# Two-bank PSUM tiles, small operations moved from ScalarE to VectorE, and the first FFN block in two halves, in a top-k attention and SwiGLU kernel

## The chip, the cores and the metric

The kernel runs on one core of one Trainium2 chip. The metric is the device time in microseconds (us) of one execution, and less is better. Engines are named as in the profile: PE (TensorE matmuls), PEld (TensorE weight loads), DVE (VectorE), ACT (ScalarE), POOL (GpSimd) and SP (SyncE, which issues nearly all DMAs).

## The reference

Two parts, one after the other. B=8 batches, H=8 heads, S=576 tokens, D=64, and an FFN with 512 and 1536 columns.

```python
scores = scale * (q @ k.T)                       # per batch and head, 576 x 576
kth    = np.partition(scores, -32)[..., -32]     # the 32nd largest of each row
attn   = softmax of scores, those below kth left out, with eps 1e-9 in the sum
x      = (attn @ v), heads side by side          # (4608, 512)
out    = (silu(x @ w_gate) * (x @ w_val)) @ w_out
```

q, k and v are float32. The three weight matrices are float64 in memory, and the kernel has to round them to float32 itself.

## The kernel before, in words

**Attention units.** A unit is one batch, one tile of 128 query tokens and one pair of heads. There are 8 x 5 x 4 = 160 units. Of each five query tiles the last has 64 tokens: it is worked as "one head" (the two heads share the partitions), so its unit has half of the work. A unit goes through these functions: `scores` (PE matmuls into PSUM, ACT copies to `sc`), `select` (top-32 on DVE: four rounds of MAX8, with three rounds of MATCH_REPLACE8 between them, for each head 7 operations), `penalize` (ACT: `top`, Relu; POOL: `bias`, subtract), `weigh` (ACT: Exp with its row sum, then the 1e-9), `normalize` (DVE reciprocal, ACT multiply), `turn` (PE transposes of `e` into `etps`, ACT copies to `et`) and `values` (PE matmuls into `av`, ACT copies to `xT`, for two units at a time). `prep` transposes q and k of a head pair once for each batch.

**The main loop.** Iteration n runs `select` of unit n, `penalize` and `weigh` of unit n-1, `normalize` and `turn` of unit n-2, and in even iterations `values` of units n-4 and n-3 and the `scores` of units n+1 and n+2. The program is emitted in one order, and the last lines of the kernel tie each engine to that order. So each engine runs its own list strictly in order, and waits where an operand or a buffer isn't ready.

**FFN blocks and pieces.** The 4608 tokens are 18 blocks of 256. `feed(kb)` is a generator that emits a block in pieces. A piece of the two products is 4 matmuls of 256 columns; on the chip each is two records (fp32 goes in two passes). ACT reads the products out of PSUM (Tanh, scale, add, copy), through a list `on_act`; POOL multiplies them, through `on_pool`. Blocks 1 to 17 then take 42 matmuls of 256 columns with differences of the output weights; block 0 takes the output weights as they are (`o_ps`, matmuls of 512 columns, 12 for each 128 tokens). A block can start when all heads of its tokens are in `xT` (`done`). In each iteration `share(n)` gives the number of pieces that may be emitted, and `pieces(k)` puts them at three places of the iteration, with what is left at its end. When no block is ready, nothing is emitted.

**Rounding the weights.** `rounded` treats a piece of 128 x 512 float64 weights: a DMA into `w` (three buffers), three ACT operations (L114 Abs of the high words, L116 the low words, L117 sign), a DVE shift (L121), and on POOL an integer add (L122) and the product with the sign (L123). There are 36 pieces: 24 for w_gate and w_val, 12 for w_out. `weights` is stepped from the main loop by `rounding(1)`, in the six `select` operations in the middle of an iteration, five times in six: 5 steps for each iteration of a full unit, 2 steps to a piece, so 2.5 pieces in an iteration. `ready[0]` counts the pieces that are rounded; `need` in `feed` steps the generator on by itself if a product is to be emitted before its weights.

**PSUM.** Five single banks `ps_t` serve scores, transposes, `av` and `prep`; three banks `ps_f` serve the FFN.

## Time and profile before

| what | before |
|---|---|
| median of 3 runs (lowest to highest) | 1851.85 us (1851.02 to 1856.61) |
| the profiled execution, its own time | 1851.39 us |
| its span in the profile | 1849.6 us |
| PE busy | 1703.3 us, 92% of the span |
| DVE busy | 1452.7 us, 79% |
| ACT busy | 1422.8 us, 77% |
| POOL busy | 1042.9 us, 56% |

The busy shares are means over stages that differ. Sections of the page: (1) engines, (2) 40 slices of the span, each digit a busy share in tenths, (4) the chain of work that ended last, (5) groups of instructions by line, with the mean time of one and the idle time before them. A timeline line gives start, duration, engine, line, operation, output and inputs, the number of merged instructions, and in brackets the idle time before it and what ended it. A duration holds the whole latency of an instruction; in a row of like instructions the distance from one start to the next is shorter.

### The profile page before, as it was taken

The numbers are of one execution on the slowest core, as the hardware profiler recorded it, in microseconds if no ns is written. First come the engines' busy times: TensorE is split into PE (matmuls) and PEld (weight loads), VectorE is DVE, ScalarE is ACT, GpSimd is POOL, SyncE is SP. The second block draws the span as 40 slices with busy tenths as digits, with TensorE's granted clock in tenths as the row PEclk, the third lists the DMA queues.
The fourth block names the chain that finished last, engine by engine and source line by source line (L and its number), as shares of the span: only waits on it lengthen the run. The fifth ranks groups of instructions, "written<-read, shape, count | busy, mean of one in ns | idle before, by whom it ended". The sixth has DMA issues, their size and how long they took to land.

```text
span 1849.6 us, 31170 instructions
## 1 busy us (share of the span) xinstructions
PE 1703.3 (92%) x11012; PEld 1401.3 (76%) x11012; DVE 1452.7 (79%) x3084; ACT 1422.8 (77%) x3329; POOL 1042.9 (56%) x1058
## 2 busy tenths in 40 slices
PE   4448899899999999999999999999999999999999
PEld 3336668687888878887888877887788878788878
DVE  6886888997998788887988877887888888788300
ACT  6898788788788787788887886878787877787632
POOL 4777755545575636564556535565556554556444
PEclk7668999899999999999999999999999999999999
DMA  6433130001200020001200020000300010000000
GB/s 181 118 91 92 34 79 14 12 1 31 63 1 13 12 68 14 12 1 28 65 13 1 12 68 25 1 13 2 90 1 13 1 43 25 1 12 12 1 12 12
DMA packets 109309, 59.70 MB, mean 32 GB/s; under 512 B 88544, under 2 KB 96992, under 8 KB 109152
## 3 DMA queue, kind: packets, MB, share of 16 engines
q1 hardware_dynamic: 108016, 57.37, 11.9%
q8 instruction: 87, 1.43, 0.3%
q14 instruction: 70, 0.57, 0.1%
q10 hardware_dynamic: 1136, 0.33, 0.1%
HBM read 48.23 MB, written 9.44 MB: 31 GB/s over the span
## 4 chain that ended last, share of the span: by engine, by line
PE 71%; ACT 15%; POOL 8%; issue 2%; DMA 1%; DVE 1%; SPq 1%; POOLq 0%; ACTq 0%
PE f L477 36%; PE av L421 8%; PE x_ps L563 8%; PE s L308 6%; PE etps L387 5%; PE y_ps L563 5%; POOL e L351 3%; ACT e L360 2%; ACT e L348 2%; ACT e L375 2%; ACT sc L313 2%; PE s L294 1%; ACT et L388 1%; PE kqps L263 1%; POOL size L122 1%
## 5 line engine op out<-in xcount | busy, mean ns | idle before, releaser
L328 DVE MAX8 m<-e 128x8 f32<-128x576 f32 x864 | 615.2, 748 | 3.3
L351 POOL TENSOR_TENSOR e<-sc,e 128x576 f32<-128x576 f32 x288 | 403.1, 1419 | 329.9 <-ACT e L348 329.9
L332 DVE MATCH_REPLACE8 e<-m,e 128x576 f32<-128x576 f32 x576 | 423.9, 742 | 0.0
L477 PE MATMUL f<-xT,wg 128*128 128x256 f32 x1728 | 403.7, 383 | 0.0
L477 PE MATMUL f<-xT,wv 128*128 128x256 f32 x1728 | 403.4, 383 | 0.0
L477 PEld LDWEIGHTS f<-xT,wg 128*128 128x128 f32 x1728 | 325.3, 192 | 51.4 <-issue 8.1
L477 PEld LDWEIGHTS f<-xT,wv 128*128 128x128 f32 x1728 | 325.9, 192 | 50.4 <-issue 8.3
L505 POOL TENSOR_TENSOR h<-h,half_g 128x512 f32<-128x512 f32 x108 | 137.9, 1277 | 227.2 <-ACT h L504 226.4
L387 PE MATMUL etps<-ident,e 128*128 128x128 f32 (+1 forms) x1312 | 189.9, 287 | 78.6 <-ACT e L375 63.3
L360 ACT ACTIVATE e<-e,bias 128x576 f32<-128x576 f32 x288 | 221.2, 771 | 49.6 <-POOL e L351 46.1
L387 PEld LDWEIGHTS etps<-ident,e 128*128 128x128 f32 (+1 forms) x1312 | 157.9, 147 | 117.4 <-ACT e L375 84.5
L328 DVE MAX8 m<-sc 128x8 f32<-128x576 f32 x288 | 203.5, 744 | 45.0 <-ACT sc L299 25.3
L308 PE MATMUL s<-kqT 64*128 64x288 f32 x1024 | 180.8, 460 | 39.6 <-ACT sc L313 24.2
L348 ACT ACTIVATE e<-sc,top 128x576 f32<-128x576 f32 x288 | 209.4, 769 | 5.2
L332 DVE MATCH_REPLACE8 e<-m,sc 128x576 f32<-128x576 f32 x288 | 211.9, 742 | 0.0
L375 ACT ACTIVATE e<-e,tot 128x576 f32<-128x576 f32 x288 | 208.8, 770 | 0.0
L510 POOL TENSOR_TENSOR h<-h,val 128x512 f32<-128x512 f32 x108 | 137.8, 1276 | 106.3 <-ACT val L509 94.9
L388 ACT COPY et<-etps 128x512 f32<-128x512 f32 (+1 forms) x448 | 183.3, 490 | 7.3 <-PE etps L387 6.5
L313 ACT COPY sc<-s 128x288 f32<-128x288 f32 x512 | 164.3, 403 | 15.6 <-PE s L308 15.6
L308 PEld LDWEIGHTS s<-kqT 64*128 64x128 f32 x1024 | 102.8, 197 | 86.6 <-ACT sc L313 30.0
L421 PE MATMUL av<-et,v 128*64 128x128 f32 (+1 forms) x2560 | 158.4, 267 | 0.0
L421 PEld LDWEIGHTS av<-et,v 128*64 128x64 f32 x2560 | 136.8, 140 | 7.5 <-ACT top L344 3.4
(74 smaller groups left out, 2000.3 us busy)
## 6 DMA issues: line engine op xcount, KB each, us to landing
v<-in_v_dram SPq DMA_DIRECT2D x32, 256.0 KB, 3.2
kq_in<-in_k_dram SPq DMA_DIRECT2D x63, 128.0 KB, 2.8
kq_in<-in_q_dram SPq DMA_DIRECT2D x63, 128.0 KB, 3.0
w<-in_moe_w_gate_dram SPq DMA_DIRECT2D x12, 512.0 KB, 3.7
w<-in_moe_w_val_dram SPq DMA_DIRECT2D x12, 512.0 KB, 3.7
w<-in_moe_w_out_dram SPq DMA_DIRECT2D x12, 512.0 KB, 3.6
out_dram<-o SPq DMA_DIRECT2D x38, 128.0 KB, 2.4
out_dram<-o SPq DMA_DIRECT2D x16, 256.0 KB, 2.4
```

Source lines behind the costliest of these rows:

```text
L308: nc.tensor.matmul(ps[:, 0:half], slab[d, q0 : q0 + P], slab[d, k0 : k0 + half])
L328: nc.vector.max(m[:, t, 8 * r : 8 * r + 8], cur[:, hs])
L332: nc.vector.match_replace(e[:, hs], m[:, t, 8 * r : 8 * r + 8], cur[:, hs], LOWEST)
L348: nc.scalar.activation(e[:, hs], sc[:, hs], AF.Relu, bias=top[:, t : t + 1], scale=-BIG)
L351: nc.gpsimd.tensor_tensor(e[:, hs], sc[:, hs], e[:, hs], ALU.subtract)
L360: nc.scalar.activation(e[:, hs], e[:, hs], AF.Exp, bias=bias[:, t : t + 1], scale=scale, accum_out=tot[:, t : t + 1],)
L375: nc.scalar.mul(e[:, hs], e[:, hs], tot[:, t : t + 1])
L387: nc.tensor.transpose(ps[0:kl, c * P : (c + 1) * P], e[:, k0 : k0 + kl], ident[:])
L388: nc.scalar.copy(et[0:kl, c0 : c0 + cn, :], ps[0:kl, 0 : cn * P].rearrange("p (c j) -> p c j", c=cn),)
L421: nc.tensor.matmul(av[d, i, 0:ql], weights_, moving, start=c == (0 if last else J), stop=c == (J if last else J - 1),)
L477: nc.tensor.matmul(ps[:, i, :], w[:, kc, m * P : (m + 1) * P], x[:, kc, :], start=(kc == 0), stop=(kc == KC - 1),)
L563: nc.tensor.matmul(ps, lhsT, T[i][m], start=m == 0, stop=m == MQ - 1)
```

## The change

PSUM: `ps_t` becomes two tiles of two banks, and a single bank `ps_1` is added for `av`, the ninth transpose and the last rows of `prep`. The scores of one head lie in one two-bank tile and are copied by one ACT operation of 576 columns instead of two of 288; eight transposes lie in one tile and are copied by one operation of 1024 columns instead of two of 512.

Off ACT: `top` (now two DVE operations at the end of `select`), the addition of 1e-9 (now two DVE operations ahead of the reciprocal), and the sign operation of the rounding. The rounded weight is now put together on DVE, by one operation that takes the sign bit of the high word and ORs it to the sum (L123 of the new kernel); it stands one step later in `weights`, and the product on POOL is gone.

FFN: block 0 becomes two halves of 128 tokens. Half 0 may start when its own 128 tokens are in `xT`. A piece is emitted only when `ready` covers its weights; otherwise `piece` returns without emitting.

```diff
-    ps_t = ctx.enter_context(tc.tile_pool(name="ps_t", bufs=5, space=PSUM))
+    ps_t = ctx.enter_context(tc.tile_pool(name="ps_t", bufs=2, space=PSUM))
+    ps_1 = ctx.enter_context(tc.tile_pool(name="ps_1", bufs=1, space=PSUM))
...
-        nc.scalar.activation(size[:], high, AF.Abs, scale=2.0**-112)
+        nc.scalar.mul(size[:], high.bitcast(FP32), 2.0**-112)
         nc.scalar.mul(low, low.bitcast(U32), 2.0**-29)
-        nc.scalar.sign(high, high)
         yield
         bits = size[:].bitcast(I32)
         nc.vector.tensor_single_scalar(bits, bits, 3, ALU.logical_shift_left)
         nc.gpsimd.tensor_tensor(bits, bits, low, ALU.add)
-        nc.gpsimd.tensor_tensor(dst, size[:], high, ALU.mult)
+        yield
+        nc.vector.scalar_tensor_tensor(
+            dst.bitcast(I32), high, SIGN, bits, ALU.bitwise_and, ALU.bitwise_or
+        )
...
-        lags = (5, 2, 0)
+        lags = (6, 5, 2, 0)
...
-            ready[0] = max((n - 5) // 2 + 1, 0)
+            ready[0] = max((n - 6) // 2 + 1, 0)
...
+        def keep(ps, t):
+            nc.scalar.copy(
+                sc[:, t * S : (t + 1) * S].rearrange("p (i k) -> p i k", i=2), ps[:, :, 0:half]
+            )
...
-            for i, ps in banks:
-                nc.scalar.copy(sc[:, i * half : (i + 1) * half], ps[:, 0:half])
+            for hh in range(2):
+                keep(ps[hh], hh)
...
+                top = small.tile([P, 2], FP32, tag="top", name="top")
+                for t in range(nh):
+                    nc.vector.tensor_scalar_mul(
+                        top[:, t : t + 1], m[:, t, TOP_K - 1 : TOP_K], BIG
+                    )
...
-        nc.scalar.mul(top[:, 0:nh], m[:, 0:nh, TOP_K - 1], BIG)
...
-        nc.scalar.activation(tot[:, 0:nh], tot[:, 0:nh], AF.Identity, bias=eps[:])
...
+        for t in range(nh):
+            nc.vector.tensor_scalar_add(tot[:, t : t + 1], tot[:, t : t + 1], EPS)
         nc.vector.reciprocal(tot[:, 0:nh], tot[:, 0:nh])
...
+        nc8 = J if last else 2 * J
+        ps = ps_t.tile([P, 2, 512], FP32, tag="t", name="etps")
+        one = ps_1.tile([P, 512], FP32, tag="u", name="e1ps")
+        for c in range(nc8):
+            nc.tensor.transpose(wide[:, c * P : (c + 1) * P], e[:, c * P : (c + 1) * P], ident[:])
+        nc.tensor.transpose(one[0:kl, 0:P], e[:, k0 : k0 + kl], ident[:])
+        nc.scalar.copy(
+            et[:, 0:nc8, :], wide[:, 0 : nc8 * P].rearrange("p (c j) -> p c j", c=nc8)
+        )
+        nc.scalar.copy(et[0:kl, nc8, :], one[0:kl, 0:P])
...
-        av = ps_t.tile([P, 2, P], FP32, tag="t", name="av")
+        av = ps_1.tile([P, 2, P], FP32, tag="u", name="av")
...
+    def feed_half(t):
+        x = xT[0]
+        cols = slice(t * P, (t + 1) * P)
+        def product(w, g, then):
+            ps = ps_f.tile([P, 4, P], FP32, tag="f", name="f")
+            for i in range(4):
+                m = 4 * g + i
+                while ready[0] < 4 * (m // 2) + (2 if w is wg else 4):
+                    yield None
+                for kc in range(KC):
+                    nc.tensor.matmul(ps[:, i, :], w[:, kc, m * P : (m + 1) * P], x[:, kc, cols], ...)
+                if i == 3:
+                    on_act.append(lambda: then(ps))
+                if i % 2 == 1:
+                    yield 1
+        # 3 x (gate, value), then 12 o_ps matmuls of 512 columns, each behind its own ready
...
-    todo = list(range(NBLK))
+    todo = [(0, 0), (0, 1)] + [(kb, None) for kb in range(1, NBLK)]
...
-                if not todo or done.get(todo[0], 0) < NHP * BLK:
+                kb, t = todo[0]
+                if done.get(kb, 0) < NHP * (P if t == 0 else BLK):
                     return 0
...
             cost = next(current[0], 0)
+            if cost is None:
+                return 0
```

## The prediction, made before the changed kernel was run

> **What bounds the kernel now.** I read the page's engines, then the windows (busy time by stretch), the waits, and the timelines of DVE, POOL and PE. Windows, with PE, PEld, DVE, ACT and POOL busy in that order, then granted clock:

> ```profile
> 25.00:150.00 125.00, 55.87 (x322) 39.97 (x323) 107.09 (x230) 108.62 (x240) 93.46 (x77) 0.61 0.41 118
> 400.00:1700.00 1300.00, 1262.70 (x8399) 1049.35 (x8398) 1096.58 (x2331) 1039.73 (x2463) 723.17 (x756) 0.99 0.09 22
> ```

> Two stages. From 400 to 1700 us PE is busy 97%: its work sets the time, and DVE and ACT have 16 to 20% to spare. Before 150 us PE is half idle, since no FFN block is ready; the iterations go at the pace of DVE and ACT. Now the early stage on DVE (iteration 6 starts at 85.32, 7 at 99.54, 8 at 111.13):

> ```profile
> 85.32 1.40 DVE L328 MAX8 m<-sc 128x8 f32<-128x576 f32 x2
> ...
> 91.05 0.99 DVE L121 TENSOR_SCALAR size<-size 128x512 int32<-128x512 int32 x1 [0.77 <-ACT size L114]
> ...
> 95.76 0.43 DVE L121 TENSOR_SCALAR size<-size 128x512 int32<-128x512 int32 x1 [2.32 <-ACT size L114]
> ...
> 104.57 0.41 DVE L121 TENSOR_SCALAR size<-size 128x512 int32<-128x512 int32 x1
> 104.90 0.09 DVE L332 MATCH_VALUE_LOAD e<-m,e 128x8 f32 x1
> ...
> 111.13 1.41 DVE L328 MAX8 m<-sc 128x8 f32<-128x576 f32 x2
> ```

> Two iterations take 25.8 us. A shift holds DVE 0.33 us (104.57 to 104.90). The rest is select, and waits for ACT.

> At iterations 28 and 29 no FFN block is ready, and here both engines can be read bare:

> ```profile
> 355.62 0.66 PE L387 MATMUL etps<-ident,e 128*128 128x128 f32 x4 [0.26 <-ACT e L375]
> 358.40 1.42 PE L387 MATMUL etps<-ident,e 128*128 128x128 f32 x5 [2.12 <-ACT sc L313]
> 362.74 2.18 PE L387 MATMUL etps<-ident,e 128*128 128x128 f32 x9 [2.92 <-ACT e L375]
> ...
> 372.27 3.72 PE L477 MATMUL f<-xT,wg 128*128 128x256 f32 x16
> ```

> PE idles here (7.3 us with two gaps not shown), and DVE starts iterations at 349.16, 358.87, 368.57: 9.70 us each, with no wait. So 9.70 us is DVE's own price of a full iteration, and this place resets what went before it.

> **What the change moves.** The instruction order of both programs on PE shows the pieces of each iteration. Before: none to iteration 9, then 31 in iterations 10 to 15. After: 12 by the end of 9 (half 0 starts in 6), 5 in 10 to 13 (its output pieces, as w_out gets rounded), 11 in 14 and 15: 28 in all. From 28 on both programs emit the same pieces. So the early start ends 3 pieces behind at iteration 16; these 3 come in iteration 27. The change can pay only by making iterations 0 to 27 shorter, or PE's waits later.

> **Rounding, the term that decides.** Per iteration there are 2.5 weight pieces. ACT loses a sign operation (0.56 us from start to start), POOL a product (1.29). DVE gains an operation, and with it a wait. In the new DVE order a piece goes: shift, one select operation, sign-OR. The sign-OR waits for POOL's add, which waits for the shift. From POOL's timeline:

> ```profile
> 16.11 1.30 POOL L122 TENSOR_TENSOR size<-size,w 128x512 int32<-128x512 int32 x1 [14.83 <-ACT sc L313]
> ```

> The shift before it ran from 15.55 to 15.97, so the add starts 0.14 us after the shift's end and takes 1.30; with another 0.15 back to DVE, the sign-OR can start 2.0 us after the shift's start. DVE gets there after 0.33 + 0.70 us: a wait of 1.0 us. Behind it on DVE is the rest of select, and behind that ACT's Relu of the next iteration. SP too: the DMA for the piece three later needs this buffer and now waits for the sign-OR, with loads of k, q and v behind it; it lands in 3.7 us and ACT needs it about one half-iteration later, so I price this at nothing (uncovered, 1 to 3 us an iteration, as ACT's waits for such DMAs are today). The sign-OR itself isn't in the trace: at least the shift's 0.33, at most 1.19 (the shift at 181.50, under a POOL add); I take 0.59, MATCH_REPLACE's 0.66 start to start scaled from 576 to 512 columns. The wait lies between 0 (the add is over) and 2.4 (a subtract of 1.42 us ahead on POOL).

> [...]

> **DVE's iteration after:** 9.70, and 0.83 for 2.5 shifts; two of 2.5 pieces meet the wait (the other's sign-OR falls into the next iteration), 2 x (1.0 + 0.59) = 3.18; 0.5 x 0.59 = 0.30; two `top` and two 1e-9 operations, 0.07 each like MATCH_VALUE_LOAD, or 0.15 where chained like RECIPROCAL: 0.45. Sum 14.5 us. Before it was 12.6 (23.36 to 137.0 over nine), of which 1.8 were waits for ACT, and those should go: ACT loses 2.5 x 0.56, and 0.21 + 0.24 + 0.16 for 1e-9, `top` and wider copies, 2.0 of some 11 us. (The copies from start to start: 288 columns 0.29, 512 columns 0.48, so 0.05 fixed and 0.83 ns a column; four of 288 against two of 576 saves 0.11, two of 512 against one of 1024 saves 0.05.) Where PE bounds, these ACT savings are worth nothing: ACT waits for PE there anyway.

> In iteration 6 POOL also gets an FFN product between two adds, which waits for Tanh. The first such one before:

> ```profile
> 154.25 1.28 POOL L505 TENSOR_TENSOR h<-h,half_g 128x512 f32<-128x512 f32 x1 [4.06 <-ACT h L504]
> 155.49 1.30 POOL L122 TENSOR_TENSOR size<-size,w 128x512 int32<-128x512 int32 x1
> ```

> DVE didn't care then; now it does: +4 us.

> **The sum.** Start of iteration 16: 10.7, iteration 0 with two such pieces 15.5, fifteen at 14.5 = 217.5, less 1.6 as 15 has fewer steps, +4: 246.1, against 226.9 before: +19.2. Before, PE was 6.3 us behind DVE there (its last `o_ps` ends at 233.1); after it should be 1 behind: -5.3. Iterations 16 to 27 are PE's, with 3 pieces more at 1.73 us: +5.2. The idle of 28 and 29 swallows those 5.2; two DVE iterations cost 0.4 more each: +0.8. Block 3 starts 14.7 us later than 372.3.

> **The halves on PE.** A record of 128 columns loads weights for half the work. The nearest row, transposes of 128 columns with fresh weights each, at 605.27, runs nine in 0.98 us: 0.109 each, and 256 columns take 0.216. So no cost; at worst the mean weight load of 0.192 sets the pace, 16 x 0.084 = 1.3 us a piece, and 11 pieces lie where PE is busy: +15.

> **PSUM, 130 iterations.** Today four transposes (0.44 us) run before the first copy of scores is needed; with two tiles all nine wait for it. That matters where the pieces between are the short ones of the output stage, 30% of 64 iterations: 64 x 0.3 x 0.45 = 8.6. In `prep` the single-bank transpose waits for the copy of the ninth, about 0.4 x 28 = 11 at most. Against this PE waits for ACT some 26 us in 400 to 1700 ("PE etps L387 <- ACT e L375: 8.9" and others), and ACT's queue gets 0.6 us shorter: perhaps 10 to 15 back. I take +4, from -15 to +60.

> Sum 14.7 + 4 = +18.7 on the profiled execution's 1851.4 (span 1849.6 and 1.8 around it; the median is 1851.85): **1870 us**.

> **Rivals.** (a) Faster: the add hides. If POOL, rid of its product, ends the add while DVE is at its select operation, the iteration is 12.5 and iteration 16 starts at 212: -15, and -4.4 at 28, none of the +4: 1832. The waits for ACT of today (31 us on L121) speak for it; the 1.30 us of the add against 0.70 of cover speaks against. It decides at a wait of 0.4 us, an iteration of 13.25. (b) Two tiles are too few: 1 us lost in each of 64 even iterations, 1850 + 15 + 64: 1930. For it: PE waits today for these copies; against: under 10 us of it is left after 400. (c) Weight loads bind the halves: 1885. (d) It doesn't do what it says: the head start and the longer iterations cancel, and the reset at 28 hides the rest: 1852.

> **How the numbers follow.** My forecast with (c) has 0.56 (1857 to 1892), (a) 0.24 (1830 to 1846), (d) 0.10, (b) 0.10. Half of (a) and (b) may be left out: 1835 to 1895; my forecast's own range is 1857 to 1892. A difference under 0.3%, 5.5 us, is about what a measurement here can't tell from none. Faster 0.25, same 0.09, slower 0.66.

> **What would show it.** DVE iterations 1 to 14 near 14.5 us, with about 1 us "<-POOL size" before the sign-OR, some 29 times; iteration 16 near 246; no wait of L121 for ACT; PE idle in 25 to 150 down; 400 to 1700 shifted but equally dense; half pieces at 1.73 us. Wrong if the early iterations are under 13.25, or if PE is under 95% busy after 400.

## The result, and the profile after

The changed kernel takes 1900.3 us (median of 4 runs, 1899.7 to 1900.4) against 1851.5 of the kernel before: a ratio of 1.0256, 95% interval 1.0238 to 1.0274. The direction was forecast, the size was not: 49 us instead of 19, which is 5 us above the wider of its two ranges (1835 to 1895). The profiled spans are 1898.6 and 1849.6 us, so +49.0 is what has to be explained.

The two windows of the prediction, columns as there:

```profile
25.00:150.00 125.00, 70.25 (x435) 57.51 (x435) 108.42 (x254) 85.02 (x159) 55.53 (x49) 0.84 0.38 106
400.00:1700.00 1300.00, 1260.31 (x8246) 1037.32 (x8245) 1124.58 (x2721) 951.97 (x1865) 703.82 (x732) 0.98 0.09 22
```

PE has more to do in the early stretch (70 us busy, 56 before), as the halves were to bring. From 400 to 1700 it is still busy 97%, but with 8246 matmul records where there were 8399, and at a clock of 0.98 instead of 0.99: less work in the same busy time. The prediction's sign, "busy under 95% after 400", could not see this, for low clock counts as busy: in one window below PE is busy for 3.38 of 3.41 us at a clock of 0.50.

**The early stage is as forecast.** DVE's timeline of iteration 6, which starts at 99.34, and the start of iteration 7:

```profile
99.34 1.41 DVE L333 MAX8 m<-sc 128x8 f32<-128x576 f32 x2
...
105.08 0.42 DVE L120 TENSOR_SCALAR size<-size 128x512 int32<-128x512 int32 x1
...
105.48 0.74 DVE L337 MATCH_REPLACE8 e<-m,e 128x576 f32<-128x576 f32 x1
106.96 0.69 DVE L123 SCALAR_TENSOR_TENSOR wv<-w,size 128x512 int32<-128x512 int32 x1 [0.73 <-POOL size L121]
107.57 0.75 DVE L333 MAX8 m<-e 128x8 f32<-128x576 f32 x1
...
113.18 0.69 DVE L123 SCALAR_TENSOR_TENSOR wg<-w,size 128x512 int32<-128x512 int32 x1 [3.87 <-POOL size L121]
...
116.76 1.41 DVE L333 MAX8 m<-sc 128x8 f32<-128x576 f32 x2
```

Shift, one select operation, then the wait for POOL's add (L121), then the sign-OR: 0.61 us from its start to the next one's (106.96 to 107.57), forecast 0.59. The 3.87 is POOL's FFN product ahead of the add (it starts at 110.61, after a wait for ACT, and the add at 111.85), forecast as +4. The waits on DVE and PE in the whole span (us in total, times, longest):

```profile
DVE wg L123 <- POOL size L121: 10.6, 10, 3.9
DVE wv L123 <- POOL size L121: 9.8, 10, 1.8
DVE wo L123 <- POOL size L121: 6.9, 9, 0.9
...
PE klps L258 <- ACT et L406: 18.7, 28, 2.4
PE kqps L266 <- ACT kqT L271: 8.3, 18, 4.7
```

That is 27.3 us in 29 sign-OR waits (forecast: about 1 us, some 29 times). Iteration 16 starts at 243.4 (forecast 246.1, before 226.9).

**The rest is at the batch boundaries.** From iteration 30 on, the delay grows from 22 to 48 us, in steps of about 5 us where iterations 20k-2 to 20k+3 pass, and hardly at all between. There `prep` of the next batch runs, and its two lines in the list above are new. PE's timeline at one boundary of the changed kernel (start, duration, operation, records, and the idle before it):

```profile
683.22 0.27 PE L402 MATMUL e1ps<-ident,e 128*128 128x128 f32 x1
683.33 0.60 PE L266 MATMUL kqps<-ident,kq_in 128*128 128x128 f32 x4
686.35 0.45 PE L258 MATMUL klps<-ident,kq_last 128*128 128x128 f32 x1 [2.42 <-ACT et L406]
686.84 1.11 PE L266 MATMUL kqps<-ident,kq_in 128*128 128x128 f32 x4
687.88 2.13 PE L302 MATMUL s<-kqT 64*64 64x288 f32 x8
...
697.65 3.09 PE L558 MATMUL f<-xT,wv 128*128 128x256 f32 x8
700.57 1.89 PE L558 MATMUL f<-xT,wg 128*128 128x256 f32 x8
```

`klps` needs the single bank, which the ninth transpose (`e1ps`) still holds: PE stands 2.42 us until ACT has copied it. Behind it four transposes take 1.11 us instead of 0.60, and eight FFN records (the four matmuls of a piece) 3.09 instead of 1.89. The granted clock shows why. In this trace it has only two values, 1.00 and 0.50, and every stretch at one of them, from one change to the next, lasts a whole number of times 3.41 us (1 to 62). So it is in all eighteen traces of this case, each on a grid of its own, and the half-clock times of the table below are whole multiples of it too, from 1 (3.4 us) to 15 (51.2 us). These windows lie on the grid of this trace (PE, PEld, DVE, ACT, POOL busy, then the clock):

```profile
683.00:686.41 3.41, 0.99 (x10) 0.75 (x8) 3.27 (x9) 3.41 (x8) 1.10 (x1) 1.00 0.00 0
686.41:689.82 3.41, 3.38 (x13) 1.57 (x13) 3.27 (x7) 2.01 (x5) 0.85 (x3) 0.50 0.15 33
689.82:693.24 3.42, 3.42 (x50) 2.85 (x48) 1.31 (x3) 1.49 (x3) 1.09 (x2) 1.00 0.66 149
693.24:696.65 3.41, 1.80 (x14) 1.06 (x10) 1.36 (x5) 3.20 (x9) 0.00 (x0) 1.00 0.07 15
696.65:700.06 3.41, 3.32 (x10) 2.87 (x11) 3.27 (x7) 2.27 (x6) 0.83 (x1) 0.50 0.25 56
```

Where the wait leaves PE busy for 29% of a window (0.99 of 3.41 us), the whole next window has half the clock, and so it is behind the one with 53% (1.80). The wait is paid for twice: once as idle, once as slower matmuls behind it.

### The profile page after: what moved, and what is told of

Same layout as the page of the kernel before. It is cut to its first block, busy times and chain, and to the rows that moved or that the text cites. A ratio compares the mean times of both kernels' runs of the same rounds, so it can differ in the third digit from the quotient of the medians.

```text
span 1898.6 us, 31385 instructions
## 1 busy us (share of the span) xinstructions
PE 1743.4 (92%) x11204; PEld 1424.7 (75%) x11204; DVE 1536.9 (81%) x3695; ACT 1313.4 (69%) x2557; POOL 994.1 (52%) x1022
## 4 chain that ended last, share of the span: by engine, by line
PE 74%; ACT 7%; POOL 4%; issue 2%; DVE 1%; POOLq 0%; ACTq 0%
PE f L558 36%; PE av L434 8%; PE x_ps L616 8%; PE s L313 7%; PE etps L400 5%; PE y_ps L616 5%; POOL e L362 2%; PE s L302 2%; ACT et L403 1%; ACT e L371 1%; ACT e L359 1%; PE f L489 1%; PE kqps L266 1%; ACT e L387 1%; PE o_ps L529 1%
## 5 line engine op out<-in xcount | busy, mean ns | idle before, releaser
L558 PE MATMUL f<-xT,wv 128*128 128x256 f32 x1632 | 381.5, 384 | 0.0
L558 PE MATMUL f<-xT,wg 128*128 128x256 f32 x1632 | 380.7, 383 | 0.0
L558 PEld LDWEIGHTS f<-xT,wv 128*128 128x128 f32 x1632 | 308.8, 192 | 47.9 <-issue 7.9
L558 PEld LDWEIGHTS f<-xT,wg 128*128 128x128 f32 x1632 | 307.3, 192 | 47.6 <-issue 8.0
L585 POOL TENSOR_TENSOR h<-h,half_g 128x512 f32<-128x512 f32 x102 | 130.0, 1274 | 219.1 <-ACT h L584 219.1
L400 PE MATMUL etps<-ident,e 128*128 128x128 f32 x1152 | 167.8, 287 | 70.7 <-ACT e L387 41.5
L400 PEld LDWEIGHTS etps<-ident,e 128*128 128x128 f32 x1152 | 139.1, 147 | 107.1 <-ACT e L387 56.0
L313 PE MATMUL s<-kqT 64*128 64x288 f32 x1024 | 191.3, 466 | 24.3 <-ACT sc L293 22.6
L387 ACT ACTIVATE e<-e,tot 128x576 f32<-128x576 f32 x288 | 209.2, 774 | 0.0
L293 ACT COPY sc<-s 128x576 f32<-128x576 f32 x288 | 170.2, 637 | 50.4 <-PE s L313 38.4
L403 ACT COPY et<-etps 128x1024 f32<-128x1024 f32 (+1 forms) x160 | 147.9, 924 | 36.5 <-PE etps L400 36.4
L313 PEld LDWEIGHTS s<-kqT 64*128 64x128 f32 x1024 | 105.0, 202 | 80.6 <-ACT sc L293 29.1
```

The costliest lines, as they stand in the source:

```text
L293: nc.scalar.copy(sc[:, t * S : (t + 1) * S].rearrange("p (i k) -> p i k", i=2), ps[:, :, 0:half])
L313: nc.tensor.matmul(ps[hh][:, i, 0:half], slab[d, q0 : q0 + P], slab[d, k0 : k0 + half])
L387: nc.scalar.mul(e[:, hs], e[:, hs], tot[:, t : t + 1])
L400: nc.tensor.transpose(wide[:, c * P : (c + 1) * P], e[:, c * P : (c + 1) * P], ident[:])
L558: nc.tensor.matmul(ps[:, i, :], w[:, kc, m * P : (m + 1) * P], x[:, kc, :], start=(kc == 0), stop=(kc == KC - 1),)
```

## The experiments

My theory from this reading: the early stage costs what was forecast, and the prediction's PSUM term is wrong. The rivals: two two-bank tiles are too few everywhere; the sign-OR's wait costs more than forecast; the halves cost.

**One part of the change at a time**, each on the kernel before.

`e1_round`: the new rounding alone.

```
- nc.scalar.sign(high, high);  nc.gpsimd.tensor_tensor(dst, size[:], high, ALU.mult)
+ yield;  nc.vector.scalar_tensor_tensor(dst..., high, SIGN, bits, bitwise_and, bitwise_or)
+ lags = (6, 5, 2, 0)
```

> The kernel before with the new rounding alone (sign-OR on DVE behind POOL's add, one step later). Theory A (the changed kernel loses its time in two places: DVE's wait for POOL's add while weights are rounded, and prep's single PSUM bank at the batch boundaries): DVE iterations 1 to 9 near 14.0 us instead of 12.6, about 1 us of waiting ahead of most sign-ORs; iterations 10 to 15 are held by PE and ACT anyway, so +8 to +18 in all, 1860 to 1870. Theory B (the loss is DVE's heavier iteration and the halves): under +6, below 1858.

Measured 1858.7 us, ratio 1.0028 (1.0018 to 1.0038), between the two expectations. Iteration 16 starts 10.8 us later; the whole is 5 us longer.

`e2_halves`: the halves and the gating on `ready` alone.

```
- todo = list(range(NBLK))
+ todo = [(0, 0), (0, 1)] + [(kb, None) for kb in range(1, NBLK)]    # with feed_half
```

> The kernel before with the first block in halves and pieces gated by ready, nothing else. Theory A: early iterations stay near 12.6 us, since no DVE operation waits for POOL; pieces move into PE's idle time, the start of iteration 16 comes 5 to 12 us earlier, 3 pieces (5.2 us) are owed later: 1843 to 1853. Theory B: the half pieces cost PE and hold up POOL and ACT: 1860 or more.

Measured 1857.2, ratio 1.0019 (1.0008 to 1.003), again between the two: a small cost, no gain.

`e3_psum`: the two-bank tiles and `ps_1` alone.

```
- ps_t bufs=5 of one bank
+ ps_t bufs=2 of two banks, ps_1 bufs=1; prep, scores, turn, av as in the change
```

> The kernel before with the two-bank tiles and the single bank alone. Theory A: nothing early, but 4 to 5 us lost at each of seven batch boundaries (klps waits for the copy of the ninth transpose, then PE runs on a lower granted clock): +25 to +38, 1877 to 1890. Theory B: PE's waits don't add up, below 1860.

Measured 1897.4, ratio 1.0247 (1.0207 to 1.0288): +44 us alone, nearly the whole loss of the change, and above both expectations.

`e4_small`: `top` and the 1e-9 on DVE, alone.

```
- nc.scalar.mul(top...);  nc.scalar.activation(tot..., AF.Identity, bias=eps[:])
+ nc.vector.tensor_scalar_mul(top...) at the end of select
+ nc.vector.tensor_scalar_add(tot..., EPS) ahead of the reciprocal
```

> The kernel before with top and the 1e-9 on DVE, nothing else. Theory A: DVE's bare iteration 10.15 instead of 9.70, hidden where PE bounds; early iterations about the same (ACT 0.45 us shorter, DVE 0.45 longer): 1848 to 1857. Theory B: DVE's heavier iteration costs in every batch: 1865 or more.

Measured 1829.6, ratio 0.9866 (0.9851 to 0.988): 24 us *faster*, which neither expectation had. Four of PE's waits for ACT from 370 to 1740 us make 25.9 us in the kernel before:

```profile
PE etps L387 <- ACT e L375: 8.9, 14, 1.8
PE kqps L263 <- ACT et L388: 6.0, 3, 2.0
PE s L308 <- ACT et L388: 5.9, 5, 2.3
PE etps L387 <- ACT sc L313: 5.1, 7, 0.8
```

In this kernel they are

```profile
PE etps L392 <- ACT e L380: 4.3, 11, 1.2
PE kqps L261 <- ACT et L393: 3.9, 3, 1.7
PE s L306 <- ACT et L393: 3.3, 5, 1.7
PE etps L392 <- ACT sc L311: 2.4, 6, 0.5
```

together 13.9. Even in the stage that PE bounds, ACT's queue is in PE's path at a few places.

**Parts taken together or taken out.** `n2_psum_small`: before, with the two-bank tiles and the small operations. `n1_nopsum`: the changed kernel without the two-bank tiles.

```
n1_nopsum, on the changed kernel:
- ps_t bufs=2 of two banks, ps_1 bufs=1
+ ps_t bufs=5 of one bank; prep, scores, turn, av as before
```

> The changed kernel without the two-bank tiles: new rounding, small operations on DVE, halves. Theory A, if the parts add (+5, -24, +4 on 1853): 1833 to 1843. Theory B, if the gain of the small operations is spent once DVE carries the rounding too: 1850 or more.

> The kernel before with the two-bank tiles and the small operations on DVE, nothing else. If the parts add (+44, -24): 1870 to 1876. If the gain of the small operations can't be had with two tiles: 1885 to 1898, and this is where the 18 us between the sum of the parts (+29) and the whole change (+47) lie.

Measured 1842.0, ratio 0.9932 (0.9917 to 0.9946), and 1880.3, ratio 1.014 (1.0125 to 1.0155). The first is what its theory A said, the second lies between its two. So the two-bank tiles cost 58 us inside the change, 51 on top of the small operations and 44 alone: they are the loss. The table sums six stretches of eight iterations (from the start of iterations 36, 56, ... 136), in which the preps lie; every stretch has the same records of PE to within four in all of these kernels, the fillers of two of them left out. "Half clock" is the time in these stretches at a granted clock of 0.50, in which a record of 256 columns takes 0.427 us from start to start instead of 0.216 (medians of the changed kernel); so half of it is about what the clock can have cost. The table is read from lines of this form; the changed kernel:

```profile
sum 484.41, PE 451.12 PEld 358.64 DVE 386.26 ACT 338.18 POOL 228.41; mean PE 75.19 PEld 59.77 DVE 64.38 ACT 56.36 POOL 38.07
```

`n1_nopsum`:

```profile
sum 440.30, PE 423.48 PEld 345.06 DVE 383.98 ACT 338.04 POOL 227.75; mean PE 70.58 PEld 57.51 DVE 64.00 ACT 56.34 POOL 37.96
```

| kernel | six stretches, us | PE busy (fillers apart) | PE idle | half clock | PE's waits in prep, 370 to 1720 us |
|---|---|---|---|---|---|
| before | 457.8 | 430.3 | 27.5 | 17.1 | 6.0 |
| e4_small | 440.2 | 423.4 | 16.9 | 3.4 | 3.9 |
| n1_nopsum | 440.3 | 423.5 | 16.8 | 3.4 | 3.9 |
| changed kernel | 484.4 | 451.1 | 33.3 | 47.8 | klps 16.9, second kq group 2.0 |
| n2_psum_small | 484.8 | 451.4 | 33.4 | 47.8 | klps 16.9, second kq group 2.2 |
| e3_psum | 498.0 | 452.8 | 45.2 | 51.2 | klps 23.5, second kq group 1.9 |
| m2_spread | 475.8 | 441.7 | 34.1 | 27.3 | klps 17.4, second kq group 2.0 |
| m1_klast | 465.4 | 430.0 | 35.4 | 13.7 | second kq group 20.7 |
| m5_prep | 450.8 | 425.5 | 25.3 | 10.2 | k1ps 10.9 |
| e5_psum_prep | 463.8 | 428.4 | 35.4 | 13.7 | k1ps 15.7 |
| m7_fill | 502.5 | 429.8 (+28.8) | 43.9 | 23.9 | filler 29.6 |
| m8_fill_first | 479.2 | 428.4 (+24.9) | 25.9 | 13.7 | klps 5.6, second kq group 5.9 |

Between `n1_nopsum` and the changed kernel lie 44.1 us: 27.6 of PE busy, with the same records, and 16.5 of idle. Of the 27.6 the clock explains some 22, half of the difference in half-clock time; where the other 5 or 6 come from stays open. Each row is one profiled run: that of `e3_psum` took 1911.9 us and that of `m8_fill_first` 1901.1, 15 and 7 above their medians, and that of `m1_klast` 1879.7, 5 below.

**Which wait.** `m1_klast`, on the changed kernel: `klps` goes behind both kq groups.

```
-        for n, at in ((0, R), (None, S), (1, S + 2 * R)):
+        for n, at in ((0, R), (1, S + 2 * R), (None, S)):   # and the yield behind n == 0
```

> The changed kernel, with the single-bank transpose of prep (klps) moved behind both groups of kq transposes, so that the copy of the ninth transpose is over when PE gets there. Theory A (single bank at the batch boundary is the main loss of the late stage): the 17 to 24 us of klps waits go, and with them some of the low granted clock: 1870 to 1885 instead of 1900. Theory B (the loss is in the two tiles that the scores and the eight transposes share): within 6 us of 1900.

Measured 1884.9, ratio 1.0169 (1.0152 to 1.0186): 15 us back. The `klps` wait is gone, but the second kq group now waits for the copy of the first, out of the same two-bank tile (20.7 us in 16 times, the longest 2.9). Idle did not shrink in the six stretches (35.4), and yet PE busy fell by 21.1: the gain is mostly clock (some 17 us by the half-clock column).

`m5_prep`, on the changed kernel: both groups that go together share the two-bank tile, and the later one has a bank of its own.

```
+        for n, at in ((0, R), (1, S + 2 * R)):
+            if n == 0: ps = both[:, 0]
+            else:
+                yield
+                ps = ps_1.tile(..., name="k1ps")
+            ...            # n == 0: klps into both[:, 1, 0:P], ahead of the copies
```

> The changed kernel with prep laid out differently: the first kq group and the last rows share the two-bank tile (all five transposes before the first copy), and the second kq group goes, one fetch step later, into the single bank. My theory (at each batch boundary PE waits for ACT copies that share a PSUM tile, and then runs at a lower granted clock): the waits of klps for the copy of the ninth transpose (18.7 us) and of the second kq group for the first copy (8.3 us) go, and part of the low clock with them: 1865 to 1880. Rival A (the cost is the wait of the nine etps transposes for the copies of scores, out of only two two-bank tiles): the boundaries stay as they are, 1885 to 1900. Rival B (the wait only moves, to the second kq group behind the copy of the ninth transpose): 1880 to 1890, with a wait of some 20 us on the new kq line.

Measured 1860.7, ratio 1.0045 (1.0028 to 1.0061): 40 of the 49 us back, more than my theory's best. The `klps` wait is gone, the second kq group (`k1ps`) waits for the ninth transpose's copy instead, 10.9 us in 370 to 1720. The six stretches:

```profile
sum 450.75, PE 425.49 PEld 346.80 DVE 384.17 ACT 336.15 POOL 228.73; mean PE 70.91 PEld 57.80 DVE 64.03 ACT 56.03 POOL 38.12
```

33.7 us less than in the changed kernel, 25.6 of them PE busy, of which the clock explains some 19. Rival A is refuted (no boundary stayed as it was), though its wait, of the `etps` transposes for copies of scores, is still there: 11.6 us in 370 to 1720 as in the changed kernel, 4.6 in `n1_nopsum`. Rival B holds for some 11 us.

`e5_psum_prep`: the kernel before with the two-bank tiles, and prep in this layout.

```
+ e3_psum's edit, with the prep of m5_prep in place of the change's
```

> The kernel before with the two-bank tiles and the single bank alone, and prep in the mended layout. If prep's layout is what failed in my PSUM sum, what is left is near the +4 of the prediction (etps 8.6, less ACT's savings): 1855 to 1866, some 35 to 40 us under the 1897.4 of the two-bank tiles alone. Rival (two two-bank tiles are too few for scores and etps too, and only the rest of the change hides that): 1872 to 1890.

Measured 1869.5, ratio 1.0084 (1.0069 to 1.0099): between the two expectations. The prep layout is 28 of the 44 us; 16 are left, with 15.7 us of `k1ps` waits in 370 to 1720. The rest of the two-bank tiles is not free, nor is it the 64 us of the prediction's rival (b).

**Do the idles take the clock down?** `m7_fill`, on the changed kernel, puts work in the idle's place:

```
+                for f in range(8):      # ahead of klps
+                    nc.tensor.transpose(both[:, 1, ...], kq_last..., ident[:])
```

> The changed kernel with eight extra transposes in each prep, right ahead of the transpose of the last rows (klps) that waits for an ACT copy; their result is overwritten by the second kq group, so only PE's time changes: 8 x 0.109 = 0.87 us in each of the 28 preps behind the first ones, 24 us more of work, of which some 17 lie in the 18.7 us that PE waits there today. My theory (the short idles are what takes the granted clock down, and so costs 29 us of PE busy time in the seven boundary windows): work in place of the idle keeps the clock up, so that the same matmuls get 10 to 25 us back, and the kernel is faster with more work: 1876 to 1892, boundary windows' clock 0.98 to 1.00. Rival (the clock falls for another reason, such as the dense stretch before, or a rhythm of its own): 1903 to 1915, clocks as before, 0.92 to 0.98.

Measured 1924.6, ratio 1.0376 (1.0359 to 1.0394): above both expectations, and a miss of the design. The filler writes into the tile whose first half ACT is copying, so it waited itself and filled nothing:

```profile
PE kqps L259 <- ACT kqT L277: 38.2, 32, 2.9
```

`m8_fill_first`: the same eight transposes ahead of the first kq group.

```
+ for f in range(8): nc.tensor.transpose(both[:, 1, ...], kq_last..., ident[:])
  for n, at in ((0, R), (None, S), (1, S + 2 * R)):
```

> As the kernel with eight extra transposes in each prep (0.87 us of PE, 24 us in 28 preps), but ahead of the first kq group, where no copy of their own tile is under way: in the other place they waited for it themselves (29.6 us) and filled no idle. Here they push the klps transpose back by 0.87 us, towards the end of the copy that it waits for (0.67 us on average). My theory (the short idle takes the clock down): klps waits under 6 us instead of 17, PE busy without the extra records falls by 15 to 29 us in the seven boundary windows, time 1876 to 1895. Rival (the clock falls for another reason): the idle goes into the filler one for one and PE busy without it stays at 528: 1900 to 1912.

Measured 1894.6, ratio 1.0223 (1.0202 to 1.0243): with 256 transposes more, 6 us faster than the changed kernel, at the upper end of my theory's range. Its waits in prep:

```profile
PE kqps L272 <- ACT kqT L277: 10.1, 20, 1.8
...
PE klps L264 <- ACT et L412: 5.6, 6, 1.6
```

The `klps` wait falls from 18.7 to 5.6 us, and in the six stretches PE busy without the extra records from 451.1 to 428.4, half-clock time from 47.8 to 13.7. So in this trace work in place of the wait does bring the clock back. That the *sum* of idle sets the clock is refuted by the table: `m1_klast`, `e5_psum_prep` and `m7_fill` idle as much as the changed kernel or more, and have 14 to 24 us at half clock.

How the clock went with PE's busy share can be counted over the eighteen traces together. From 370 to 1720 us they have 6972 windows of the grid at full clock. Of the 71 in which PE is busy under 45%, 70 are followed by a window at half clock; of the 108 from 45 to 65%, 21 are; of the 6793 above that, 4. In the traces of the kernel before and of the changed kernel alone it is 10 of 11, 5 of 13 and 1 of 741. The length of a wait alone doesn't tell: at 908.29 in the changed kernel PE waits 1.26 us for a copy of scores, within one window (busy for 1.72 of its 3.42 us), and the next window has half the clock; at 1123.03 the same wait of 1.26 us lies in two windows (busy for 3.12 and 2.00 us), and the clock stays at 1.00. Another near miss is `m1_klast`, from 689.25 to 692.67, where PE is busy for half of the window (waits of 1.26 and 0.77 us) and the clock stays at 1.00:

```profile
689.25:692.67 3.42, 1.71 (x14) 1.43 (x14) 1.91 (x6) 2.66 (x7) 0.00 (x0) 1.00 0.06 14
692.67:696.08 3.41, 3.41 (x19) 3.02 (x18) 3.27 (x8) 2.34 (x6) 1.42 (x1) 1.00 0.38 86
```

The grid lies elsewhere in each trace (an edge is at 686.41 in that of the changed kernel and at 658.23 in that of the kernel before, 8.26 windows apart), so part of what one trace shows of the clock is chance. `m2_spread`, below, still has the `klps` waits (17.4 us) and yet only 27.3 us at half clock; the other three kernels with them have 47.8 to 51.2.

**The early wait.** `m2_spread`, on the changed kernel: the five rounding steps go over all 14 select operations, so that two or three of them stand between a shift and its sign-OR.

```
-                due[0] += 5 / 6 if beside else 0
+                due[0] += 5 / 14
```

> The changed kernel, with the five rounding steps of an iteration spread over all fourteen select operations instead of the middle six, so that two to three select operations lie between a shift and its sign-OR. Theory A (DVE waits for POOL's add): the 27 us of DVE waits behind POOL go to under 8, early iterations 12.3 to 12.9 us instead of 14.5, iteration 16 starts 15 to 25 us earlier; of this 8 to 20 us reach the end: 1880 to 1892. Theory B (the head start and the wait cancel at the reset): under 5 us.

Measured 1880.3, ratio 1.014 (1.0114 to 1.0167): 20 us back, inside theory A's range, though two of its steps fell short: the waits went to 14.9 us, not under 8, and iteration 16 starts 14.0 us earlier, not 15 to 25. In the profiled run, 1876.7, the lead is 11.4 us at iteration 44 and 23.3 at the last one; the second half comes from less half-clock time at the boundaries (27.3 us, not 47.8), where the edit changes nothing. The four runs lie at 1876.4, 1876.7, 1884.0 and 1886.0.

`m6_prep_spread`: `m5_prep` and this together.

> The prep of the run before, and the five rounding steps of an iteration spread over all 14 select operations. If the early wait (27 us of sign-OR waits, worth 20 us alone) and the boundary cost are independent, the two savings add: 20 us below the kernel with the new prep alone, 1845 to 1862. Rival: one idle of PE takes the place of the other and the sum is under 10 us: 1858 to 1870.

Measured 1852.6, ratio 1.0 (0.9989 to 1.0011), which is the kernel before again: only 8 us under `m5_prep`, so the two savings do not add. Iteration 16 starts 13.3 us earlier than in `m5_prep`, iteration 28 10.0, the last 9.3. So the early part is had in full (14.0 in `m2_spread`); what is missing is the gain of clock behind it, for the two kernels have the same half-clock time, 10.2 us in the six stretches.

`b2_nopsum_spread`: `n1_nopsum` with the spread (the same one-line edit). `b1_small_spread`: the kernel before with the small operations, the new rounding and the spread, without two-bank tiles and halves.

> The changed kernel without its two-bank tiles, with the rounding steps spread over all 14 select operations. My theory: 20 us under the 1842.0 of the same kernel without the spread, as the spread took 20 us off the whole change: 1820 to 1830. Rival (without the two-bank tiles ACT is quick enough that the wait is hidden at iteration 28): 1835 to 1843.

> The kernel before with top and 1e-9 on DVE, the new rounding, and the rounding steps spread over all 14 select operations; no two-bank tiles and no halves. My theory: the new rounding cost its 5 us through the sign-OR's wait alone; spread out, that wait is covered and ACT's lost sign operation counts: 1818 to 1830, at or under the 1829.6 of the small operations alone. Rival (DVE's 0.6 us for each sign-OR is what counts, no matter where it lies): 1832 to 1840.

Measured 1830.6, ratio 0.9877 (0.9857 to 0.9896), between its two expectations, and 1824.0, ratio 0.9844 (0.9828 to 0.9861), as my theory said. The spread is worth 11 us without the two-bank tiles, 8 with a mended prep, and 20 in the change as it is, some half of that, by its profiled run, through the clock. `b1_small_spread` beats both kernels, by 29 and 76 us, and `e4_small` by 6. The halves and the gating, the one difference between `b1` and `b2`, cost 7 us.

**What the small operations save.** `e6_top`: the kernel before with only `top` on DVE.

```
- nc.scalar.mul(top[:, 0:nh], m[:, 0:nh, TOP_K - 1], BIG)
+ nc.vector.tensor_scalar_mul(top...) at the end of select
```

> The kernel before with only top moved to DVE (1e-9 stays on ACT). The two moves together gave 24 us. Theory (top stood at the head of ACT's chain select, top, Relu, behind which the exponentials and copies wait; 1e-9 only costs ACT its time): two thirds or more of it, 1832 to 1840. Rival (only ACT's time counts, 0.24 of 0.45 us): about half, 1839 to 1844; or all of it comes from 1e-9: 1849 to 1855.

Measured 1841.3 (1834.2 to 1843.7), ratio 0.9932 (0.9906 to 0.9958): 12 of the 24 us. That fits the rival, ACT's time (0.24 of 0.45 us), better than the place of `top` in ACT's chain, but does not show it: the four runs scatter over 10 us. The other move brings clock too: half-clock time in the six stretches is 17.1 us in `e6_top`, as before, and 3.4 in `e4_small`.

## Why the prediction was wrong

**What held.** The early iterations: 14.5 us in the mean of 1 to 14 without iteration 6 (forecast 14.5), a wait of 0.94 us (1.0), a sign-OR of 0.61 (0.59), DVE's bare iteration 10.16 (10.15), POOL's insertion in iteration 6 a wait of 3.9 (+4). Rival (a) is out: 14.5, and the line was drawn at 13.25. What POOL added to the length of the sign-OR itself is small: two of 36 took over 1.7 us and two about 1.0, against a median of 0.69, some 3 us in all. These four, and no other, start while a POOL operation with two inputs runs: the one at 126.47 (1.74 us) under a product from 126.40 to 127.66. In the kernel before a shift did the like: 0.41 us at 104.57, with nothing on POOL, and 0.99 at 91.05, under a product from 90.47 to 91.76.

**The sum to block 3 held as well**, once the two-bank tiles are out of the way. `n1_nopsum` has the new rounding, the halves and the small operations; its block 3 begins

```profile
386.88 3.72 PE L553 MATMUL f<-xT,wg 128*128 128x256 f32 x16
```

14.6 us later than the 372.27 of before; forecast was 14.7. In the changed kernel it begins

```profile
395.33 3.72 PE L558 MATMUL f<-xT,wg 128*128 128x256 f32 x16
```

23.1 later. So the sum of the early stage holds, and 8.5 us of the two-bank tiles' cost fall before block 3: 1.6 until iteration 16, 4.6 at the batch boundary of iterations 16 to 23, most of the rest at 28 and 29.

**The step that failed is the PSUM term**, +4 from -15 to +60. It was a difference of two, and both were mis-sized:

| term | forecast, us | measured, us |
|---|---|---|
| up to block 3, without two-bank tiles | +14.7 | +14.6 (n1_nopsum) |
| cost of the two-bank tiles | 8.6 + 11 at most, with the next row taken as +4 | +59.2 (span after less span of n1_nopsum) |
| ACT's savings and the rest, behind block 3 | -10 to -15 | -24.8 (span of n1_nopsum 1839.4, so -10.2, less 14.6) |
| sum | +18.7 | +49.0 |

The cost first. The prediction saw the right wait ("in `prep` the single-bank transpose waits for the copy of the ninth") and put it at 0.4 x 28 = 11 at most; it is 18.7, 0.67 each, and another 8.3 for the second kq group, which the prediction did not have: out of two separate banks no copy of the first group was in its way. But idle is the smaller part. The prediction priced a wait at its own length, and had nothing for the clock behind it. Of the 39.7 us by which `m5_prep` has the shorter span, 33.7 lie in the six stretches: 8.0 are idle, and 25.6 are the same matmuls taking longer, some 19 of them at half clock. What remains of the cost is 1858.9 - 1839.4 = 19.5, of which 10.5 lie in the same stretches. The "8.6" for the nine transposes is in it: their wait for copies of scores is 7.0 us longer than in `n1_nopsum` (11.6 and 4.6 in 370 to 1720), so that term was about right.

The savings next. "Where PE bounds, these ACT savings are worth nothing" is wrong as a rule: alone they gave 24 us, half of it from `top`. At a few places PE waits for ACT although PE is busy 97% of the stage. In `e4_small` the six stretches are 17.6 us shorter than before: 10.7 of idle and 6.9 of PE busy, which is what 13.7 us less at half clock are worth.

**The other rivals.** (b), 1 us in each of 64 even iterations, has the right size by luck and not the mechanism: between boundaries hardly anything is lost, and a change to `prep` alone gives 40 us back. (c), weight loads that bind the halves, +15: the halves and the gating cost 4 us alone, and 7 on top of `b1_small_spread`; that weight loads are what costs is not shown. (d), 1852, is out.

## What to carry to other kernels

A buffer plan is priced at the places where its rarest user runs: five interchangeable banks had absorbed a `prep` every 20 iterations, and one bank of a pool of its own made PE stand there. A wait of PE costs more than its length if the granted clock falls behind it (here 2.42 us of idle, and then 3.41 us at a clock of 0.50), so look at the clock in windows of a few us next to the wait, laid where the trace shows it to change, and not at busy shares of a long stage, which count slow matmuls as work. Where one profile decides, ask how much of it is where the grid happened to lie. And "PE bounds this stage" does not make another engine's savings worthless: look in the stage for the few places where PE still waits for that engine, and multiply.
